# Ones through TensorE in the opening, maxima scaled on ScalarE, remainders of x on GpSimd

## The chip, the cores and the metric

The kernel runs on one core of a Trainium2 chip. The core has a matrix engine (TensorE, PE in the profile, with its weight loads PEld), three engines for elementwise work (VectorE or DVE, ScalarE or ACT, GpSimd or POOL), and a queue from which it issues DMAs (SyncE or SP). The metric is the device time of one execution in microseconds. The kernel before took 577.8 us as the median of three runs (575.98 to 578.51).

## The reference

Eight batches of windowed attention with 8 heads feed a mixing layer. Cut to what matters:

```python
scores = scale * np.matmul(q, k.transpose(0, 1, 3, 2))      # (8, 8, 576, 576), masked to a window
scores = scores - np.max(scores, axis=-1, keepdims=True)     # of 32 keys (plain, or every 4th of 128)
attn = np.exp(scores)
attn = attn / (np.sum(attn, axis=-1, keepdims=True) + 1e-09)
x = np.matmul(attn, v)                                       # heads side by side: (8, 576, 512)
theta = x @ w_theta
zr, zi = x * np.cos(theta), x * np.sin(theta)
y = np.einsum('ts,bsd->btd', w_tok_r, zr) + np.einsum('ts,bsd->btd', w_tok_i, zi)
u = x + y
out = u + np.maximum(u @ w_ch, 0.0)
```

q, k and v are fp32; the four weights are float64 in the kernel's inputs and are unpacked on the chip.

## The kernel before

**Stages.** A batch b has four pairs of heads. For a pair, `scores` multiplies blocks of 32 queries of both heads with the 64 keys in reach, into two PSUM banks (tag "s", two of them: a group of 5 blocks and one of 4), VectorE takes the row maxima, ScalarE the exponentials with their sums (line 485 or 504), VectorE the reciprocals of the sums (L507, L508) and GpSimd the product with them (L510). VectorE then transposes the probabilities in blocks of 32 (`turn`, L525; batch 0 does it on TensorE, `flip`), `pv` multiplies with v into the bank "v", ScalarE copies the result out as x (L581), and `x_split` makes from x a rounded part (ScalarE, L593) and a remainder (L597 for 64 columns, L599 for 512), since products are made in three passes of fp32r: rounded by rounded, rounded by remainder, remainder by rounded. `theta` multiplies x by w_theta, `trig` makes cosine and sine (L787 to L796, L698, L705), multiplies them by x (L750) and splits the results into zh (L641 or L644) and zl (L646). A `token` unit y(b, d, g) is 27 matmuls over nine z tiles (kt) for 128 channels d and half of the rows g; its sum is added to x (L825) and split again into u. A `chan` unit c(b, e, g) is 12 matmuls over u, added by L859.

**What overlaps.** From batch 1 on TensorE works on the units of one batch while the other engines make the probabilities, x, cosine and sine of the next. Names carry batch and pair: s1_2_0 is the first score group of batch 1, pair 2, xh1_0 the split x of batch 1, pair 0; the profile leaves the numbers out.

**The opening.** Up to about 144 us the kernel loads and unpacks the weights, does batch 0 whole and the attention of batch 1. A weight tile (st_wth, st_wtk, st_wch) is loaded as float64, clipped on VectorE (L332), scaled on ScalarE (L334, L340), joined on VectorE (L342), rounded on ScalarE (L350), and its remainder made on GpSimd (L352). The four tiles of w_ch, st_wch0 to st_wch3, take turns in two buffers, whose tags are xh2 and xh3: st_wch2 is loaded when GpSimd has made late_wc0 from st_wch0, st_wch3 when late_wc1 is made. Afterwards xh1_2 and xh1_3 live in the same buffers.

**What sets the order.** Batch 0 and batch 1's attention are written as tasks with ranks (`RANK`). A planner (`Order`) with a cost for each step and engine decides, when the kernel is built, in which order each engine takes them, and this order is then fixed. A cost in a `yield` therefore moves instructions when it changes. From phase(1, 2) on the order is that of the code. TensorE's matmuls go through `pe`, which keeps them in program order. In `row_max` (batch 0, and pairs (1,2), (1,3), (2,0), (2,1), whose mask is added by TensorE) the maxima are taken group by group (L430) and, behind batch 0, scaled by -1/8 on VectorE (L438); the exponentials of the group read them as bias.

## Time and profile before

| | |
|---|---|
| median of three runs | 577.8 us |
| profiled execution, its own time | 577.82 us |
| its span, first to last instruction | 576.0 us |
| busy share: TensorE, its weight loads | 96%, 87% |
| busy share: VectorE, ScalarE, GpSimd | 66%, 60%, 39% |
| mean granted clock of TensorE | 0.988 |

A row of the timeline is: start, duration, engine, line, operation, output<-input, shapes, count; in brackets the idle time before it and who ended it. Several instructions of one form in sequence stand in one row. A row by form has the busy time and the mean of one, then the idle time before. The clock is given as a share of 2.4 GHz. Since 200 us on look alike, nearly all that differs from a full TensorE lies in the first 145 us.

### The profile page before, as it was taken

What the parts mean: (1) busy time and instruction counts of PE and PEld (TensorE: products, weight loads), DVE (VectorE), ACT (ScalarE), POOL (GpSimd) and SP (SyncE); (2) the same over time, 40 slices, a digit from 0 to 9 for tenths busy, and PEclk for the clock granted to TensorE, in tenths of its full rate; (3) what the DMA queues carried; (4) which work ended last, traced back from release to release, by engine and by line L of the source; (5) the groups of instructions that cost most, each with busy time, mean ns of one, the idle gap of its engine ahead of it and who ended that gap; (6) DMA issues with size and microseconds to landing.
All of it is one profiled execution on the core that took longest, in us unless ns stands there. A gap on an engine that the chain in (4) does not pass through costs nothing.

```text
span 576.0 us, 13996 instructions
## 1 busy us (share of the span) xinstructions
PE 550.5 (96%) x5464; PEld 501.6 (87%) x5464; DVE 378.0 (66%) x1156; ACT 345.2 (60%) x939; POOL 222.2 (39%) x206
## 2 busy tenths in 40 slices
PE   5997799999999999999999999999999999999997
PEld 4744688879999899988999899988999899989997
DVE  3879798865666668756776768756775767445112
ACT  1498967768555784369555785359556695266110
POOL 2228855525224352226324253226323353325220
PEclk9999699899999999999999999999999999999999
DMA  8991437601747046540746146550747123321002
GB/s 303 400 368 28 165 105 245 216 0 63 231 150 193 32 162 210 169 127 20 268 143 172 64 148 202 181 136 11 252 146 190 69 83 102 77 89 65 18 1 83
DMA packets 45586, 81.91 MB, mean 142 GB/s; under 512 B 3920, under 2 KB 19024, under 8 KB 45520
## 3 DMA queue, kind: packets, MB, share of 16 engines
q1 hardware_dynamic: 45520, 81.02, 43.7%
q8 instruction: 43, 0.70, 0.5%
q14 instruction: 23, 0.19, 0.1%
HBM read 64.49 MB, written 16.52 MB: 141 GB/s over the span
## 4 chain that ended last, share of the span: by engine, by line
DVE 34%; ACT 30%; PE 25%; issue 5%; POOL 2%; DMA 2%; SPq 0%; ACTq 0%; POOLq 0%; DVEq 0%
DVE pt L525 16%; PE y L850 11%; ACT P L504 11%; PE c L882 6%; PE th L685 3%; DVE P L409 3%; ACT K L698 3%; ACT K L787 3%; DVE xh L599 3%; ACT th L796 2%; ACT zh L644 2%; DVE xq L729 2%; DVE K L789 2%; ACT cos L705 2%; ACT x L581 2%
## 5 line engine op out<-in xcount | busy, mean ns | idle before, releaser
L830 POOL TENSOR_TENSOR u<-x,u 128x288 fp32r<-128x288 f32 x64 | 54.7, 858 | 184.6 <-ACT u L828 184.6
L525 DVE STREAM_TRANSPOSE pt<-P 32x288 f32<-32x288 f32 x224 | 105.1, 469 | 12.0 <-POOL P L510 8.9
L882 PE MATMUL c<-u,late_wc 128*128 128x288 f32 x768 | 110.2, 296 | 2.8 <-DVE x L859 2.8
L882 PEld LDWEIGHTS c<-u,late_wc 128*128 128x128 f32 x768 | 106.0, 188 | 6.8 <-DVE x L859 4.0
L850 PE MATMUL y<-wtkh,zh 128*128 128x288 f32 x288 | 90.3, 314 | 1.1 <-ACT zh L644 1.1
L850 PE MATMUL y<-wtkh,zl 128*128 128x288 f32 x288 | 86.2, 299 | 4.0 <-POOL zl L646 4.0
L646 POOL TENSOR_TENSOR zl<-g,zh 128x512 fp32r<-128x512 f32 x40 | 52.3, 1316 | 97.5 <-ACT zh L644 84.5
L504 ACT ACTIVATE P<-P,mx 128x64 f32<-128x64 f32 x216 | 72.0, 335 | 25.8 <-DVE mx L498 25.8
L850 PE MATMUL y<-wtkl,zh 128*128 128x288 f32 x288 | 85.9, 298 | 0.0
L828 ACT CAST u<-x 128x288 fp32r<-128x288 f32 x64 | 26.9, 429 | 86.2 <-DVE x L825 85.5
L685 PE MATMUL th<-wthh,xh 128*128 128x512 f32 x224 | 74.8, 395 | 0.3 <-DVE g L784 0.3
L850 PE MATMUL y<-late_wt_b,zh 128*128 128x288 f32 x320 | 68.1, 297 | 0.0
L825 DVE TENSOR_TENSOR x<-y,x 128x288 f32<-128x288 f32 x64 | 28.1, 448 | 53.6 <-PE y L850 53.5
L850 PEld LDWEIGHTS y<-wtkh,zl 128*128 128x128 f32 x288 | 55.1, 191 | 4.7 <-POOL zl L646 4.7
L850 PEld LDWEIGHTS y<-wtkh,zh 128*128 128x128 f32 x288 | 54.9, 191 | 4.7 <-ACT zh L644 2.3
L850 PE MATMUL y<-late_wt_a,zh 128*128 128x288 f32 x256 | 56.3, 301 | 0.0
L850 PEld LDWEIGHTS y<-wtkl,zh 128*128 128x128 f32 x288 | 55.1, 191 | 0.3 <-issue 0.3
L510 POOL TENSOR_TENSOR P<-P,sm 128x576 f32<-128x576 f32 x32 | 37.5, 1172 | 41.1 <-DVE sm L508 18.1
L850 PEld LDWEIGHTS y<-late_wt_b,zh 128*128 128x128 f32 x320 | 51.4, 189 | 0.3
L685 PEld LDWEIGHTS th<-wthh,xh 128*128 128x128 f32 x224 | 42.0, 188 | 9.2 <-DVE g L784 0.6
L850 PE MATMUL y<-late_wt_b,zl 128*128 128x288 f32 x160 | 47.4, 296 | 0.0
L581 ACT COPY x<-o 128x576 f32<-128x576 f32 x32 | 29.4, 919 | 28.4 <-PE o L617 19.1
(108 smaller groups left out, 1106.3 us busy)
## 6 DMA issues: line engine op xcount, KB each, us to landing
q<-in_qT_dram SPq DMA_DIRECT2D x32, 576.0 KB, 5.2
va<-in_vw_dram SPq DMA_DIRECT2D x30, 320.0 KB, 3.2
k<-in_kT_dram SPq DMA_DIRECT2D x28, 304.0 KB, 5.5
out_dram<-x SPq DMA_DIRECT2D x28, 288.0 KB, 2.4
vb<-in_vw_dram SPq DMA_DIRECT2D x29, 256.0 KB, 3.8
xd<-xq SPq DMA_DIRECT2D x24, 288.0 KB, 5.1
xn<-xd SPq DMA_DIRECT2D x24, 256.0 KB, 3.4
st_wtk<-in_wtk_dram SPq DMA_DIRECT2D x8, 576.0 KB, 8.8
```

Source lines behind the costliest of these rows:

```text
L409: pin(nc.vector.tensor_tensor_reduce(out=P[:, n], in0=ps[:, n - g0], in1=mskb[:, mask_of(pr, n)], op0=ALU.add, op1=ALU.max, scale=1.0, sca ...
L504: table(nc.scalar.activation(P[:, n], P[:, n], AF.Exp, bias=mx[:, n:n + 1], scale=SCALE, accum_out=sm[:, n:n + 1]))
L510: pin(nc.gpsimd.tensor_tensor(P, P, sm.unsqueeze(2).to_broadcast([128, NJ, BW]), op=ALU.mult))
L525: pin(nc.vector.transpose(pmats[b, pr][k0:k0 + QB, :, hh, QB * e:QB * e + QB], P[p0:p0 + QB, :, QB * o:QB * o + QB]))
L581: pin(nc.scalar.copy(dst, src))
L646: pin(nc.gpsimd.tensor_tensor(lo, z, hi.bitcast(F32), op=ALU.subtract))
L685: pe(nc.tensor.matmul(pt, l, r, start=(n == 0), stop=(n == 3 * NC - 1)))
L825: pin(nc.vector.tensor_tensor(x[:, ts], ps, x[:, ts], op=ALU.add))
L828: pin(nc.scalar.copy(uh[b, d][:, ts], x[:, ts]))
L830: pin(nc.gpsimd.tensor_tensor(ul[b, d][:, ts], x[:, ts], uh[b, d][:, ts].bitcast(F32), op=ALU.subtract))
L850: pe(nc.tensor.matmul(ps, l[:, cs], r, start=(n == 0), stop=(n == 3 * NK - 1)))
L882: pe(nc.tensor.matmul(ps, l[:, cs], r[:, ts], start=(n == 0), stop=(n == 3 * NC - 1)))
```

## The change

It does five things. (1) Before the first loads arrive, VectorE writes a tile of ones, and TensorE multiplies it by itself 14 times (512 columns, bf16) into the bank of "v". (2) In unit (0,0,0), ahead of the tile kt = 3, it does so eight times before the first matmul and four times before the third, which needs the remainder. (3) In `row_max` the scaling of the maxima goes from VectorE to ScalarE, for the four pairs that are not of batch 0: eight instructions. (4) In `x_split` the remainders of pairs 0 to 2 of batch 1 go from VectorE to GpSimd, as those of pair 3 already are: six instructions. (5) As costs and engines of steps change, the planner sets another order for what follows, from the scores of (1,3) on.

```diff
--- before.py
+++ after.py
@@ -38,7 +38,10 @@
 
 FG0 = {4: ("zl2", "zl6"), 0: ("zl3", "zl7"), 1: ("zh3", "zh7")}
 COS_PSUM, SIN_PSUM = True, True
+WARM_UP = 14
 KORD = (0, 4, 1, 5, 2, 6, 3, 7, 8)
+
+KEEP_BUSY = {(0, 0, 0, 3, 0): 8, (0, 0, 0, 3, 2): 4}
 TP0 = {4: "s", 0: "s", 1: "x", 2: "t", 3: "s"}
 TP = {4: "t", 0: "s", 1: "s", 2: "t", 3: "s"}
 
@@ -434,8 +437,8 @@
                                         op=ALU.subtract))
             give(*rel)
         else:
-            yield "DVE", 170
-            pin(nc.vector.tensor_scalar(mx[:, g0:g1], mx[:, g0:g1], -SCALE, None, op0=ALU.mult))
+            yield "ACT", 220
+            pin(nc.scalar.mul(mx[:, g0:g1], mx[:, g0:g1], -SCALE))
         signal(key)
 
     def scores(b, pr):
@@ -591,7 +594,7 @@
         lo, lt = hl[:, S + 64:], hl[:, S:S + 64]
         yield "ACT", act(S)
         pin(nc.scalar.copy(hi, x))
-        on = pr < 3
+        on = pr < 3 and b > 1
         eng, cost = (nc.vector, dve) if on else (nc.gpsimd, pool)
         yield "DVE" if on else "POOL", cost(64)
         pin(eng.tensor_tensor(lt, x[:, FS:], hi[:, FS:].bitcast(F32), op=ALU.subtract))
@@ -845,10 +848,16 @@
             yield None, ("wtk", g, kt // 2)
             zh, zl = zs[b, kt]
             wh, wl = (w[:, HS * (kt % 2):HS * (kt % 2) + HS] for w in wtks[g, kt // 2])
+            if (b, d, g, kt) == (0, 0, 0, KORD[6]):
+                busy = yield from bank("v", "busy")
             yield "PE", 369
-            for l, r in ((zh, wh), (zh, wl), (zl, wh)):
+            for i, (l, r) in enumerate(((zh, wh), (zh, wl), (zl, wh))):
+                for _ in range(KEEP_BUSY.get((b, d, g, kt, i), 0)):
+                    pe(nc.tensor.matmul(busy[0][:, :DM], ones[:, :128], ones, start=True, stop=True))
                 pe(nc.tensor.matmul(ps, l[:, cs], r, start=(n == 0), stop=(n == 3 * NK - 1)))
                 n += 1
+        if b == d == g == 0:
+            give(*busy[1])
         signal(("tk", b, d, g))
         go(residual(b, d, g, ps, rel), RANK["evacuate"])
 
@@ -953,6 +962,12 @@
     EA, LA, LA2 = ([(t, reserve(t)) for t in ts] for ts in (EARLY, LATE, LATE2))
     XH = {p: reserve(f"xh{p}") for p in range(NP)}
     UH = {d: reserve(f"u{d}") for d in range(NC)}
+
+    ones = cp.tile([128, DM], BF16, name="ones")
+    nc.vector.memset(ones, 1.0)
+    busy = ps_v.tile([128, 2 * DM], F32, tag="v", name="busy")
+    for n in range(WARM_UP):
+        pe(nc.tensor.matmul(busy[:, :DM], ones[:, :128], ones, start=True, stop=True))
     od.live = True
     go(first_loads(), 0)
     go(consts(), 0)
```

VectorE at the scores of batch 1, pair 2. mx1_2 are the maxima, pt1 the transposed probabilities of pair 1, x0_2 the residual. Before:

```order
L430 TENSOR_REDUCE mx1_2_906<-s1_2_0_908 128x5
L525 STREAM_TRANSPOSE pt1_109<-P1_1_724 32x9x32 x2
L438 TENSOR_SCALAR mx1_2_906<-mx1_2_906 128x5
L430 TENSOR_REDUCE mx1_2_906<-s1_2_5_940 128x4
L825 TENSOR_TENSOR x0_2_407<-y0_2_0_883,x0_2_407 128x288
L438 TENSOR_SCALAR mx1_2_906<-mx1_2_906 128x4
```

And now:

```order
L433 TENSOR_REDUCE mx1_2_936<-s1_2_0_938 128x5
L528 STREAM_TRANSPOSE pt1_126<-P1_1_741 32x9x32 x2
L433 TENSOR_REDUCE mx1_2_936<-s1_2_5_970 128x4
L828 TENSOR_TENSOR x0_2_424<-y0_2_0_913,x0_2_424 128x288
L345 SCALAR_TENSOR_TENSOR st_wtk1_2_426<-st_wtk1_2_426 128x576
L345 SCALAR_TENSOR_TENSOR st_wtk1_3_496<-st_wtk1_3_496 128x576
```

The two scalings are gone; ScalarE has each of them directly ahead of the exponentials that read it.

GpSimd from the last product of batch 1 on (P1_3). xh1_n are the remainders of x, late_wcn the weights of the channel units, u0_n the remainders of batch 0's u. Before:

```order
L510 TENSOR_TENSOR P1_3_968<-P1_3_968,sm1_3_970 128x576
L830 TENSOR_TENSOR u0_0_831<-x0_0_274,u0_0_831 128x288
L352 TENSOR_TENSOR late_wc0_1205<-st_wch0_1063,late_wc0_1205 128x512
L352 TENSOR_TENSOR late_wc1_1231<-st_wch1_1113,late_wc1_1231 128x512
L830 TENSOR_TENSOR u0_1_884<-x0_1_350,u0_1_884 128x288
L510 TENSOR_TENSOR P2_0_1165<-P2_0_1165,sm2_0_1167 128x576
L352 TENSOR_TENSOR late_wc2_1373<-st_wch2_1233,late_wc2_1373 128x512
L352 TENSOR_TENSOR late_wc3_1383<-st_wch3_1262,late_wc3_1383 128x512
L830 TENSOR_TENSOR u0_2_957<-x0_2_407,u0_2_957 128x288
L510 TENSOR_TENSOR P2_1_1277<-P2_1_1277,sm2_1_1279 128x576
L597 TENSOR_TENSOR xh1_3_1454<-x1_3_1340,xh1_3_1454 128x64
L599 TENSOR_TENSOR xh1_3_1454<-x1_3_1340,xh1_3_1454 128x512
```

And now:

```order
L513 TENSOR_TENSOR P1_3_998<-P1_3_998,sm1_3_1000 128x576
L600 TENSOR_TENSOR xh1_0_1152<-x1_0_933,xh1_0_1152 128x64
L600 TENSOR_TENSOR xh1_1_1194<-x1_1_1076,xh1_1_1194 128x64
L602 TENSOR_TENSOR xh1_0_1152<-x1_0_933,xh1_0_1152 128x512
L602 TENSOR_TENSOR xh1_1_1194<-x1_1_1076,xh1_1_1194 128x512
L355 TENSOR_TENSOR late_wc0_1250<-st_wch0_1107,late_wc0_1250 128x512
L833 TENSOR_TENSOR u0_0_861<-x0_0_291,u0_0_861 128x288
L355 TENSOR_TENSOR late_wc1_1319<-st_wch1_1129,late_wc1_1319 128x512
L513 TENSOR_TENSOR P2_0_1175<-P2_0_1175,sm2_0_1177 128x576
L833 TENSOR_TENSOR u0_1_914<-x0_1_367,u0_1_914 128x288
L355 TENSOR_TENSOR late_wc2_1426<-st_wch2_1288,late_wc2_1426 128x512
L513 TENSOR_TENSOR P2_1_1301<-P2_1_1301,sm2_1_1303 128x576
```

Four remainders stand ahead of late_wc0, and P2_0 and P2_1 have moved forward; the two remainders of xh1_2 and those of xh1_3 follow behind late_wc3.

TensorE where batch 0's channel units (c0) meet theta of batch 1 (th1_4). Before:

```order
L882 MATMUL c0_0_0_1468<-u0_0_831,late_wc0_1205 128x288 x3
L882 MATMUL c0_0_0_1468<-u0_1_884,late_wc1_1231 128x288 x3
L882 MATMUL c0_0_0_1468<-u0_2_957,late_wc2_1373 128x288 x3
L882 MATMUL c0_0_0_1468<-u0_3_1121,late_wc3_1383 128x288 x3
L690 MATMUL th1_4_1477<-wthh0_631,xh1_0_1133 128x512
L692 MATMUL th1_4_1477<-wthl0_632,xh1_0_1133 64x512
L689 MATMUL th1_4_1477<-wthl1_654,xh1_1_1123 64x512
L690 MATMUL th1_4_1477<-wthh1_653,xh1_1_1123 128x512
L689 MATMUL th1_4_1477<-wthl2_673,xh1_2_1421 64x512
L690 MATMUL th1_4_1477<-wthh2_672,xh1_2_1421 128x512
L689 MATMUL th1_4_1477<-wthl3_685,xh1_3_1454 64x512
L690 MATMUL th1_4_1477<-wthh3_684,xh1_3_1454 128x512
```

And now:

```order
L891 MATMUL c0_0_0_1499<-u0_0_861,late_wc0_1250 128x288 x3
L891 MATMUL c0_0_0_1499<-u0_1_914,late_wc1_1319 128x288 x3
L891 MATMUL c0_0_0_1499<-u0_2_987,late_wc2_1426 128x288 x3
L891 MATMUL c0_0_0_1499<-u0_3_1125,late_wc3_1470 128x288 x3
L891 MATMUL c0_1_0_1519<-u0_0_861,late_wc0_1250 128x288 x3
L891 MATMUL c0_1_0_1519<-u0_1_914,late_wc1_1319 128x288 x3
L891 MATMUL c0_1_0_1519<-u0_2_987,late_wc2_1426 128x288 x3
L891 MATMUL c0_1_0_1519<-u0_3_1125,late_wc3_1470 128x288 x3
L891 MATMUL c0_2_0_1539<-u0_0_861,late_wc0_1250 128x288 x3
L693 MATMUL th1_4_1531<-wthh0_648,xh1_0_1152 128x512
L695 MATMUL th1_4_1531<-wthl0_649,xh1_0_1152 64x512
L692 MATMUL th1_4_1531<-wthl1_671,xh1_1_1194 64x512
```

The unit c0_1_0 and the first quarter of c0_2_0, 15 matmuls, now stand ahead of th1_4; the units behind move up, so that 12 fewer remain at the end.

## Rows read from the trace of the kernel before

**Rows 1.** Busy time by stretch: us, then PE, PEld, DVE, ACT, POOL, clock, DMA.

```profile
200.00:300.00 100.00, 98.91 (x1095) 93.44 (x1094) 71.42 (x259) 62.27 (x181) 37.06 (x34) 1.00 0.49 153
```

**Rows 2.** Timeline of TensorE, first scores.

```profile
10.27 1.34 PE L468 MATMUL s<-first_k,q 128*64 128x64 f32 x20
...
18.02 0.80 PE L468 MATMUL s<-first_k,q 128*64 128x64 f32 x20
```

**Rows 3.** Timelines of SyncE and VectorE, first st_wth, and its time to landing.

```profile
11.62 0.33 SPq L325 DMA_DIRECT2D st_wth<-in_wth_dram  x1
...
23.32 0.91 DVE L332 TENSOR_SCALAR st_wth<-st_wth 128x512 f32<-128x512 f32 x1
...
DMA to landing us min/median/max: 10.1/10.1/10.1
```

**Rows 4.** Busy time by stretch, two stretches at the lower clock.

```profile
67.82:71.24 3.42, 3.42 (x17) 3.42 (x16) 1.99 (x7) 3.42 (x17) 2.81 (x4) 0.50 0.00 0
101.95:105.37 3.42, 3.42 (x30) 2.89 (x30) 2.25 (x9) 2.19 (x10) 1.25 (x1) 0.50 0.84 275
```

**Rows 5.** Timeline of TensorE, its waits in the opening.

```profile
66.79 0.40 PE L850 MATMUL y<-wtkh,zl 128*128 128x288 f32 x1 [1.11 <-POOL zl L646]
...
82.47 0.31 PE L424 MATMUL s<-mskb,idb 128*128 128x64 bf16 x5 [1.04 <-ACT P L485]
...
101.51 0.30 PE L424 MATMUL s<-mskb,idb 128*128 128x64 bf16 x2 [1.95 <-ACT P L485]
...
125.11 0.63 PE L759 MATMUL xn<-idt,x 128*128 128x128 f32 x4 [1.02 <-DVE g L750]
```

**Rows 6.** VectorE by form from 80 to 116 us: busy us, mean ns.

```profile
L599 DVE TENSOR_TENSOR xh<-x,xh 128x512 fp32r<-128x512 f32 x3 | 2.1, 687 | 0.0
L438 DVE TENSOR_SCALAR mx<-mx 128x5 f32<-128x5 f32 x4 | 1.8, 455 | 0.1
...
L438 DVE TENSOR_SCALAR mx<-mx 128x4 f32<-128x4 f32 x4 | 1.2, 312 | 0.1
...
L597 DVE TENSOR_TENSOR xh<-x,xh 128x64 fp32r<-128x64 f32 x3 | 1.1, 363 | 0.0
```

**Rows 7.** Timelines of VectorE and ScalarE, scores of batch 1, pair 2.

```profile
79.02 0.49 DVE L430 TENSOR_REDUCE mx<-s 128x5 f32<-128x320 f32 x1
...
80.83 0.31 ACT L485 ACTIVATE P<-s,mx 128x64 f32<-128x64 f32 x1 [2.35 <-DVE mx L438]
```

**Rows 8.** Timelines of VectorE and GpSimd: a long scaling, weights, remainders.

```profile
84.77 1.30 DVE L438 TENSOR_SCALAR mx<-mx 128x5 f32<-128x5 f32 x1
...
84.60 1.45 POOL L352 TENSOR_TENSOR late_wt_b<-st_wtk,late_wt_b 128x576 fp32r<-128x576 f32 x1 [0.76 <-ACT late_wt_b L350]
...
109.70 2.60 POOL L352 TENSOR_TENSOR late_wc<-st_wch,late_wc 128x512 fp32r<-128x512 f32 x2 [2.27 <-ACT late_wc L350]
...
114.21 0.84 POOL L597 TENSOR_TENSOR xh<-x,xh 128x64 fp32r<-128x64 f32 x1
115.01 1.30 POOL L599 TENSOR_TENSOR xh<-x,xh 128x512 fp32r<-128x512 f32 x1
116.27 0.81 POOL L830 TENSOR_TENSOR u<-x,u 128x288 fp32r<-128x288 f32 x1
```

**Rows 9.** The load of st_wch3: time to landing, and VectorE's first use.

```profile
DMA to landing us min/median/max: 5.6/5.6/5.6
...
105.36 0.43 DVE L332 TENSOR_SCALAR st_wch<-st_wch 128x512 f32<-128x512 f32 x1 [1.03 <-DMA st_wch<-in_wch_dram]
```

**Rows 10.** Timelines of TensorE and VectorE, end of the opening.

```profile
116.34 0.40 PE L690 MATMUL th<-wthh,xh 128*128 128x512 f32 x1
...
138.84 4.24 PE L882 MATMUL c<-u,late_wc 128*128 128x288 f32 x30
143.01 1.27 PE L468 MATMUL s<-k,q 128*64 128x64 f32 x36
...
143.86 0.22 DVE L409 CUSTOM_DVE_ANT_0 P<-s,mskb 128x64 f32<-128x64 f32 x1 [0.28 <-PE s L468]
```

## Prediction

> **What bounds the kernel now.** I read the busy time by stretch first: from 200 to 300 us TensorE is busy 98.91 of 100 us [rows 1]. The body is bound by TensorE and its work is untouched, so what the opening gives or costs, up to where batch 1's token units begin (about 144 us), comes through to the end one for one. Second, TensorE's timeline, to see where it runs slowly. The first scores of a pair, 20 matmuls, take 1.34 us at 10.27 and 0.80 at 18.02 [rows 2]; the duration says that the clock stands at its lower level (1.2 GHz) in the first, though no change of clock is recorded before it. Two later stretches of 3.42 us stand at a granted 0.50 [rows 4]; each can cost at most half of itself, 1.7 us. Third, TensorE's waits: 1.11 us for the last zl, 1.04 and 1.95 us for a score bank that ScalarE's exponentials hold, 1.02 us for a multiplication at 125 [rows 5]. The low stretches of 67.82 and 101.95 come right behind the waits that end at 66.79 and 101.51; behind the single wait of 1.04 there is none. Last, who makes TensorE wait: ScalarE had been idle for 2.35 us when the exponentials began at 80.83, for want of a scaled maximum whose reduction had begun at 79.02 [rows 7]. That is VectorE's queue.
>
> **Fourteen matmuls of ones at the start.** The trace has none; 30 channel matmuls of 288 columns take 4.24 us, 0.14 each [rows 10], so 512 columns should take about 0.25 at the higher level and 0.50 at the lower: 3.5 to 7 us, from about 1.3, beside the first loads. If the clock then stands at 2.4 GHz, the second pair still waits for its load until 10.27, but each group behind saves 0.54 us (1.34 less 0.80): two more pairs and a flip up to 17 us make about 1.8. Then the weights decide. The first st_wth is issued at 11.62 and lands 10.1 us later, about 21.9 counted from the end of the issue; VectorE uses it at 23.32 [rows 3]. So about 1.4 us passes this point. Behind it the elementwise engines work in a fixed order from loads that are there, and I carry the 1.4 through. Bounds: 0 (the clock falls again while pair 1 is awaited, some 1.2 us, which lies between the wait of 1.04 that left it up and that of 1.95 that did not) and -1.8. I take **-1.4**, since 1.2 is nearer to 1.04.
>
> **Twelve matmuls of ones in unit (0,0,0).** Eight ahead of kt 3's zh and four ahead of its zl, each lot in a wait of 1.1 us. At 0.25 they take 2.0 and 1.0 us, so zl's matmul starts about 0.5 us late, and the low stretch at 67.82 goes (up to 1.7 of TensorE's time). Neither reaches the end by itself: VectorE gets the unit's sum before its next transposes are ready either way, and what TensorE wins until 81 it waits away at the bank of 82.47. At the lower level the twelve take twice as long and the first residual is about 1 us late. I take **0**, bounds -0.3 and +1.0.
>
> **Eight scalings to ScalarE, six remainders to GpSimd.** VectorE loses 1.8 + 1.2 us of L438 and 2.1 + 1.1 us of L597 and L599 [rows 6], 6.2 us where it is the engine that others wait for. A scaling on ScalarE has no row; the nearest, an exponential over 64 columns, is 0.31 [rows 7], a bound from above, and I take 0.25. It can start where the reduction ends (79.5), not behind two transposes, so the exponentials and the bank come about 0.9 us earlier. TensorE gains the waits of 1.04 and 1.95 and the low stretches, up to 1.7 each, 6.4 in all; some 2.2 come back as waits, since it arrives earlier at the first bank than the bank does (1.9) and just ahead of the second (0.3), and 0.4 is the late zl: it reaches the channel units about 3.8 us earlier.
>
> But these need more than TensorE. st_wch3 goes into the buffer of st_wch1, once GpSimd has made late_wc1. It lands 5.6 us after its issue, and VectorE waits 1.03 us for it, until 105.36 [rows 9]; late_wc3 ends at 112.30 [rows 8]. In the new order four remainders (2 x 0.84 + 2 x 1.30 = 4.3 us) stand on GpSimd ahead of late_wc0, and on ScalarE the cast for late_wc1 stands behind nine exponentials and a copy. Taking what is queued in turn, I get late_wc1 1.0 to 2.4 us later than now. Its load then shares the queue with less, and so lands sooner after its issue: late_wc3 ends about where it does now, 111.0 to 113.5. Behind it GpSimd then has two pairs of remainders and one u, 2 x 2.14 + 0.8 = 5.1 us, where it had 4.0 (115.01 + 1.30 less 112.30) [rows 8]. The last matmul of th1_4, at 116.34 [rows 10] right behind GpSimd's last remainder, so moves **later by 1.0**, bounds -0.3 and +2.4.
>
> What remains behind that matmul gets shorter. Now it is 143.01 - 116.34 = 26.7 us to the next scores. Fifteen channel matmuls now stand ahead of th1_4: 15 x 0.14 = 2.1 us. The wait of 1.02 and a short one ahead of it go, 1.3, since VectorE's queue is then empty and takes th1_4 at once. Against this the last multiplication by a cosine stands behind five score masks, 5 x 0.15 us from start to start (0.22 each) [rows 10], and its remainder ends about 0.8 us after TensorE wants it. Tail: -2.1 - 1.3 + 0.8 = **-2.6**.
>
> Sum: -1.4 + 0 + 1.0 - 2.6 = -3.0 on the profiled execution's span of 576.0; with the 1.8 us around it that execution took 577.8, the median of the three. **574.8 us.**
>
> **A rule against the change.** VectorE's scaling at 84.77 took 1.30 us, as long as GpSimd's subtraction from 84.60 went on (1.45) [rows 8]; the mean of its kind is 0.46 [rows 6]. The page "SBUF — State Buffer" of the Trainium skill (section "Who interferes with whom") says that VectorE's two-port operations, tensor_scalar among them, and GpSimd's take a shared pair of ports as a lock for a whole instruction. The trace agrees, as far as that row goes. By that rule each of the four L332 of st_wch could wait out a remainder of 1.30, and the sum would be up to 5 us worse, an estimate of about 580. Rival (c) is the same danger, worked out from rows.
>
> **Rivals.** (a) The ones do not do what they say: the clock falls again before pair 1, the first term is 0, 576.2. For it: only matmuls of 64 columns follow, and the wait of 1.2. Against it: the wait of 1.04 did no harm. (b) The weights' chain does not bind: st_wch3 lands early, GpSimd keeps up, and the 3.8 us reach the end: -3.8 - 1.3 + 0.8 - 1.4 = -5.7, 572.1. For it: GpSimd is the least busy engine. Against it: ScalarE's queue ahead of late_wc1. (c) Slower: GpSimd's queue becomes the bound. The four remainders (4.3) come whole in front of late_wc1, and the L332 of st_wch1 and of st_wch3 wait 1.3 each behind a remainder: late_wc3 6.9 later, the last matmul of th1_4 8.0 later, +8.0 - 2.6 - 1.4 = +4.0, 581.8. It decides when GpSimd's last remainder of batch 1 ends after 120.3 (no gain left) and is slower from 123.2. For it: the 1.30 at 84.77. Against it: GpSimd stands idle in front of most of these rows now.
>
> **How the numbers follow.** About half a per cent, 2.9 us, is what a measurement of this kernel can tell from no change; the border is 574.9. Forecast 0.50, some 573.0 to 576.4, half of it on either side of the border; (a) 0.16; (b) 0.22; (c) 0.12. Faster 0.22 + 0.25 = 0.47; same 0.25 + 0.16 = 0.41; slower 0.12. The range leaves out (c) and the far end of (b): 571.0 to 578.0.
>
> **What would show it.** Right: score groups of 0.80 at 10.27; the first st_wth used near 21.9; no low stretch around 68; exponentials of (1,2) right behind their reduction; the last matmul of th1_4 near 115.9 (117.3 less 1.4), behind a remainder on GpSimd; the scores of (2,2) near 139. Wrong: groups of 1.34 at 10.27; GpSimd idle ahead of its last remainders, or with a queue there past 120; a new low stretch behind a wait for late_wc3 around 110, which I have not priced and which could cost up to 1.7.

## The result, and the profile after

The changed kernel takes 580.25 us, the median of 7 runs (578.66 to 580.83), against 577.45 for the kernel before (7 runs, 575.98 to 578.51): a ratio of 1.0046 with a 95% interval of 1.0033 to 1.0059. It is slower by about 2.7 us, where 574.8 was forecast and the range ended at 578.0. The profiled execution took 579.98, its span is 578.2, 2.1 more than that of before.

To see where the 2.1 us come from I set the start of the same instruction in the two traces side by side; "later" and "earlier" below are such differences, counted from each span's start. At the score group that starts at 18.02 in before TensorE is 1.9 earlier (16.13), VectorE uses the first st_wth 0.9 earlier, and at 31 us both are 0.3 later. VectorE is still 0.2 to 0.3 later at 81. The last matmul of th1_4 is 4.6 later, the scores of pair (2,2) 0.9. From 156 us on VectorE is 2.1 later. TensorE is 1.3 later there, since it waits less on the way, and 2.1 later only from 206 us to the end (its wait for a residual there is 0.89, in before 0.52). So the whole loss is made ahead of 156 us, and VectorE's queue carries it into the body [rows 1], which passes it on unchanged from 206 us.

**The start.** TensorE's timeline, which answers [rows 2] and [rows 3]. Columns: start, duration, engine, line, operation, tiles, count, and in brackets the idle time ahead with what ended it ("issue": nothing that the profile shows).

```profile
1.45 5.83 PE L970 MATMUL busy<-ones 128*128 128x512 bf16 x14 [1.45 <-DVE halfpi L306]
...
10.19 0.80 PE L471 MATMUL s<-first_k,q 128*64 128x64 f32 x20 [0.60 <-DMA first_k<-in_kT_dram]
...
16.76 0.86 PE L620 MATMUL o<-pt,first_v 128*64 128x64 f32 x22
18.78 0.62 PE L620 MATMUL o<-pt,first_v 128*64 128x64 f32 x14 [1.16 <-issue]
19.34 0.80 PE L564 MATMUL pT<-idt,P 64*64 64x64 f32 x20
20.07 0.29 PE L427 MATMUL s<-mskb,idb 128*128 128x64 bf16 x4
20.29 0.68 PE L564 MATMUL pT<-idt,P 64*64 64x64 f32 x16
20.90 0.69 PE L471 MATMUL s<-first_k,q 128*64 128x64 f32 x16
21.41 1.22 PE L620 MATMUL o<-pt,first_v 128*64 128x64 f32 x36
23.11 0.91 PE L564 MATMUL pT<-idt,P 64*64 64x64 f32 x22 [0.48 <-POOL P L513]
24.91 0.67 PE L564 MATMUL pT<-idt,P 64*64 64x64 f32 x14 [0.89 <-issue]
```

The ones do what they say: the score groups take 0.80. But TensorE then stops twice in the middle of 36 equal matmuls, behind the 22nd, for 1.16 and 0.89 us. Between the two stops lie 14 + 20 + 4 + 16 + 16 + 36 + 22 = 128 matmuls, each with a weight load of its own: 256 instructions. The queues (queue, kind: packets, MB, share of the DMA engines), first for 15.9 to 17.6 us, then for the whole span:

```profile
q1 hardware_dynamic: 271, 0.66, 99.5%
q8 instruction: 1, 0.02, 3.9%
```

```profile
q8 instruction: 43, 0.70, 0.5%
```

One packet of instructions is on its way just ahead of the first stop, beside loads that fill the DMA engines; another lies in 22.4 to 23.9 us, and none between 18 and 22. Over the span 43 packets of 16 KB stand against 5490 matmuls and 5490 loads, which is 255 for each. So in these traces TensorE's instructions come in packets of 256, and beside the first loads it waits for the next one. TensorE's waits list two such stops in the whole span, these two; in before none.

**Unit (0,0,0).** The last zl's matmul starts at 67.17, against 66.79 [rows 5]; the low stretch of 67.82 [rows 4] is gone, and TensorE runs into the banks at 78.34 (0.76 idle) and 81.81 (1.02 idle). VectorE is where it was.

**The weights' chain**, which answers [rows 8], on GpSimd:

```profile
97.08 1.31 POOL L355 TENSOR_TENSOR late_wc<-st_wch,late_wc 128x512 fp32r<-128x512 f32 x1 [1.67 <-ACT late_wc L353]
...
102.21 1.30 POOL L355 TENSOR_TENSOR late_wc<-st_wch,late_wc 128x512 fp32r<-128x512 f32 x1 [3.06 <-ACT late_wc L353]
...
108.28 1.30 POOL L355 TENSOR_TENSOR late_wc<-st_wch,late_wc 128x512 fp32r<-128x512 f32 x1 [2.54 <-ACT late_wc L353]
...
113.96 1.28 POOL L355 TENSOR_TENSOR late_wc<-st_wch,late_wc 128x512 fp32r<-128x512 f32 x1
...
117.76 1.27 POOL L602 TENSOR_TENSOR xh<-x,xh 128x512 fp32r<-128x512 f32 x1
```

Before, late_wc0 and late_wc1 were made one behind the other:

```profile
96.73 2.86 POOL L352 TENSOR_TENSOR late_wc<-st_wch,late_wc 128x512 fp32r<-128x512 f32 x2 [0.33 <-ACT late_wc L350]
```

late_wc1 now ends at 103.51, 3.9 later; the load of st_wch3, which waits for it, is issued at 103.54 instead of 99.6, and late_wc3 ends at 115.24, 2.9 later. GpSimd is idle ahead of three of the four and waits for casts on ScalarE. Only late_wc3 itself stands behind a queue there: its cast ended at 112.95, and GpSimd first made a product and a remainder of u, 1.0 us (0.8 in before). ScalarE's rows for st_wch0 and st_wch1, of before and then of after:

```profile
94.50 0.70 ACT L334 ACTIVATE st_wch<-st_wch 128x512 f32<-128x512 f32 x1 [1.74 <-DVE st_wch L332]
...
95.99 0.66 ACT L350 CAST late_wc<-st_wch 128x512 fp32r<-128x512 f32 x1
...
97.18 0.67 ACT L350 CAST late_wc<-st_wch 128x512 fp32r<-128x512 f32 x1 [0.53 <-DVE st_wch L342]
```

```profile
96.34 0.67 ACT L353 CAST late_wc<-st_wch 128x512 fp32r<-128x512 f32 x1 [1.01 <-DVE st_wch L345]
96.91 0.68 ACT L337 ACTIVATE st_wch<-st_wch 128x512 f32<-128x512 f32 x1
...
101.47 0.67 ACT L353 CAST late_wc<-st_wch 128x512 fp32r<-128x512 f32 x1
```

The first step on st_wch1 (L334, now L337) stood ahead of the cast for late_wc0 and now stands behind it: 94.50 becomes 96.91. VectorE's next step (L345) comes at 100.22, behind a reduction and two transposes, and the cast behind a copy and four exponentials at 101.47, 4.3 later than before.

One more step on this chain became long, VectorE's clip of st_wch3 (L335, L332 of before), and ScalarE was idle for it:

```profile
108.49 1.39 DVE L335 TENSOR_SCALAR st_wch<-st_wch 128x512 f32<-128x512 f32 x1
109.95 0.67 ACT L337 ACTIVATE st_wch<-st_wch 128x512 f32<-128x512 f32 x1 [1.75 <-DVE st_wch L335]
```

It took 0.43 in before; here it runs beside GpSimd's subtraction for late_wc2 (108.28 to 109.58). So what st_wch3 won by landing sooner, 4.6 us behind its issue and not 5.6, the clip lost again.

**What TensorE makes of it**, which answers [rows 10] and [rows 4]: its timeline, then busy time by stretch (stretch, length, busy time and count of PE, PEld, DVE, ACT, POOL, then granted clock, DMA share, GB/s).

```profile
111.90 1.63 PE L891 MATMUL c<-u,late_wc 128*128 128x288 f32 x11
115.29 4.16 PE L891 MATMUL c<-u,late_wc 128*128 128x288 f32 x16 [1.76 <-POOL late_wc L355]
...
120.97 0.39 PE L693 MATMUL th<-wthh,xh 128*128 128x512 f32 x1
...
143.87 1.27 PE L471 MATMUL s<-k,q 128*64 128x64 f32 x36
```

```profile
116.05:119.47 3.42, 3.42 (x16) 3.42 (x15) 2.46 (x6) 0.23 (x1) 2.98 (x4) 0.50 0.00 0
```

Before, all twelve matmuls of the first channel unit went through at once:

```profile
113.14 1.74 PE L882 MATMUL c<-u,late_wc 128*128 128x288 f32 x12
```

TensorE now comes to the channel units 1.2 earlier (111.90 against 113.14), does what it can, waits 1.76 for late_wc3, and behind that wait 3.42 us stand at a granted 0.50, the lower level. Counted to the last matmul of th1_4: 1.2 earlier, the wait 1.76, half of the slow stretch 1.7, and the 15 channel matmuls that now stand ahead, 2.1, make 4.4 of the 4.6.

**The cosine.** VectorE and ScalarE behind the scores of (2,2):

```profile
145.45 0.69 DVE L753 TENSOR_TENSOR K<-xn,K 128x512 f32<-128x512 f32 x1
...
146.17 0.62 ACT L647 CAST zh<-K 128x512 fp32r<-128x512 f32 x1 [1.30 <-DVE K L753]
```

In before the cast waited less:

```profile
142.64 0.62 ACT L644 CAST zh<-K 128x512 fp32r<-128x512 f32 x1 [0.25 <-DVE K L750]
```

The multiplication now starts behind five masks. VectorE's loss goes from 0.86 at the scores to 2.11 at 156 us, 1.25; TensorE's reaches 2.12 at 206.

### The profile page after: what moved, and what is told of

It is laid out like the page before. It is cut to its first block, busy times and chain, and to the rows that moved or that the text cites. A ratio compares the mean times of both kernels' runs of the same rounds, so it can differ in the third digit from the quotient of the medians.

```text
span 578.2 us, 14049 instructions
## 1 busy us (share of the span) xinstructions
PE 555.3 (96%) x5490; PEld 501.3 (87%) x5490; DVE 374.7 (65%) x1143; ACT 345.8 (60%) x947; POOL 225.8 (39%) x212
## 4 chain that ended last, share of the span: by engine, by line
DVE 27%; ACT 26%; PE 23%; issue 3%; POOL 2%; ACTq 0%; DVEq 0%; POOLq 0%
DVE pt L528 13%; ACT P L507 10%; PE y L857 10%; PE c L891 7%; PE th L688 4%; DVE P L412 3%; ACT K L701 3%; ACT th L799 2%; DVE xh L602 2%; ACT K L790 2%; ACT zh L647 2%; DVE xq L732 2%; ACT cos L708 2%; DVE K L792 2%; ACT x L584 1%
## 5 line engine op out<-in xcount | busy, mean ns | idle before, releaser
L891 PE MATMUL c<-u,late_wc 128*128 128x288 f32 x768 | 112.3, 299 | 5.0 <-DVE x L868 3.2
L891 PEld LDWEIGHTS c<-u,late_wc 128*128 128x128 f32 x768 | 107.6, 190 | 9.4 <-DVE x L868 4.3
```

What stands on the lines that cost most here:

```text
L891: pe(nc.tensor.matmul(ps, l[:, cs], r[:, ts], start=(n == 0), stop=(n == 3 * NC - 1)))
```

## The experiments

The theory after the comparison (A): the loss has two places, the late late_wc3 (a wait, and the clock that falls behind it) and the cosine behind the masks; the ones at the start gain nothing since instructions stop TensorE there. Rival (B): one of the four parts costs it all, or the order of the instructions as a whole does. Every kernel here computes the whole reference. "of before" is the median of the runs of before that were made beside it. The changed kernel was not run again beside the experiments. The before that ran beside it took 577.45, the one beside other kernels up to 578.81, so a kernel is set against the changed one by the two ratios; where the intervals of two ratios overlap, as most here do, the order of the two is not shown.

### Each part alone

e_warm, the ones at the start:

```diff
+WARM_UP = 14
...
+    ones = cp.tile([128, DM], BF16, name="ones")
+    nc.vector.memset(ones, 1.0)
+    busy = ps_v.tile([128, 2 * DM], F32, tag="v", name="busy")
+    for n in range(WARM_UP):
+        pe(nc.tensor.matmul(busy[:, :DM], ones[:, :128], ones, start=True, stop=True))
```

e_keep, the ones in the unit:

```diff
+KEEP_BUSY = {(0, 0, 0, 3, 0): 8, (0, 0, 0, 3, 2): 4}
...
+                for _ in range(KEEP_BUSY.get((b, d, g, kt, i), 0)):
+                    pe(nc.tensor.matmul(busy[0][:, :DM], ones[:, :128], ones, start=True, stop=True))
```

e_scale and e_rem, the scalings and the remainders:

```diff
-            pin(nc.vector.tensor_scalar(mx[:, g0:g1], mx[:, g0:g1], -SCALE, None, op0=ALU.mult))
+            pin(nc.scalar.mul(mx[:, g0:g1], mx[:, g0:g1], -SCALE))
```

```diff
-        on = pr < 3
+        on = pr < 3 and b > 1
```

> The kernel before with the fourteen matmuls of ones at the start alone. In the changed kernel TensorE was 1.9 us ahead at 17 us and then stood idle for 1.16 us in the middle of the group that starts at 16.76 and for 0.89 us in the middle of the one at 23.11, with nothing it waited for; 256 of its instructions lie between the two places, and each comes about 1.2 to 1.5 us behind the end of a packet of its instruction queue (16 KB, 256 instructions). Theory A (TensorE runs out of instructions, since the packets stand behind the loads): the same two gaps here, VectorE's first L345 at 26.6 as in the changed kernel (26.31 before), time +0.3 us, 577.4 to 578.2. Rival B (the prediction's step: 1.4 us pass the first weights, and are lost only further on through other parts of the change): first L345 near 24.9, time -1.4, 575.5 to 576.5.

> The kernel before with the twelve matmuls of ones in unit (0,0,0) alone. Theory A (they take the low stretch at 67.8 away, but what TensorE wins is waited away at the next score bank, and VectorE's queue does not move): VectorE's maxima of (1,2) at 79.0 as before, TensorE waits about 2.3 us at the bank of 82.47, time within 0.5 us of before. Rival B (TensorE's 1.3 us reach the units of 100 us): the scores of batch 2, pair 2, at 141.7 instead of 143.0, time -1.3 us.

> The kernel before with the eight scalings on ScalarE alone; remainders stay on VectorE. In the changed kernel the remainder late_wc1 was made 3.9 us later than before (its end 103.5, before 99.6), so the last weight tile was issued 3.9 us later and late_wc3 ended at 115.24 (before 112.30). Theory A (the order that the planner makes when the scalings move puts the weight steps behind other work on VectorE and ScalarE; GpSimd stood idle ahead of late_wc0 and late_wc1): the same here, late_wc1 ends 2.5 us or more later than before, TensorE waits for late_wc3 at its first channel unit and has a low clock behind it, time +1 to +3 us. Rival B (the remainders on GpSimd do it: four of them ahead of late_wc0, and the clips of 1.0 and 1.4 us beside GpSimd): late_wc1 ends at 99.6 to 101, no wait for late_wc3, time -1 to -4 us.

> The kernel before with the six remainders of x on GpSimd alone; scalings stay on VectorE. Theory A (order by the scalings): the weights' chain stays about where it was, late_wc1 ends at 99 to 101.5, no wait of TensorE for late_wc3 of over 0.5 us, time -1 to +0.5 us. Rival B (the remainders on GpSimd delay the weights): late_wc1 ends at 103 or later, a wait for late_wc3 and a low stretch behind it, time +1 to +3 us.

Medians 579.73, 579.73, 579.86 and 579.83 (of before 577.3); ratios 1.0039 (1.0023 to 1.0055), 1.0037 (1.0022 to 1.0052), 1.0047 (1.0032 to 1.0062) and 1.0040 (1.0026 to 1.0053). Each part alone costs 2.4 to 2.6 us, nearly as much as all four. The costs don't add, and most of what I expected of the single parts was wrong: e_warm's time lies in neither range, and only its second stop for instructions is there (0.49, behind the 22nd matmul); e_keep waits 1.54 us at the bank of 82 us where about 2.3 was expected.

The scalings alone already make late_wc1 end at 104.1 and late_wc3 at 114.4, and TensorE shows the picture of the changed kernel, in four waits instead of one, with a low stretch of its own:

```profile
116.00 3.11 PE L885 MATMUL c<-u,late_wc 128*128 128x288 f32 x12 [1.13 <-DVE x L828]
```

```profile
116.19:119.60 3.41, 3.41 (x14) 3.16 (x14) 2.27 (x5) 0.22 (x1) 1.31 (x2) 0.50 0.00 0
```

The remainders alone leave late_wc1 where it was (99.1). Their trace, the fastest of its ten runs, shows the cosine's 1.25, from 0.77 earlier at 143 us to 0.48 later at 156; late_wc3 ends 1.8 later there too (114.09), but no wait for it follows. The rest of their median I can't place. So the remainders alone cost about as much while late_wc1 stays in time.

With ones alone the loss comes between 88 and 110 us, at another place. TensorE and VectorE of e_keep:

```profile
103.30 0.43 PE L427 MATMUL s<-mskb,idb 128*128 128x64 bf16 x2 [3.46 <-ACT P L488]
```

```profile
92.55 0.43 DVE L335 TENSOR_SCALAR st_wch<-st_wch 128x512 f32<-128x512 f32 x1 [1.23 <-DMA st_wch<-in_wch_dram]
...
109.49 0.42 DVE L433 TENSOR_REDUCE mx<-s 128x4 f32<-128x256 f32 x1 [2.36 <-PE s L471]
```

```profile
102.45:109.28 6.83, 5.98 (x51) 5.15 (x50) 4.10 (x13) 5.43 (x24) 2.40 (x2) 0.50 0.55 202
```

The first st_wch lands 5.9 us after its issue (4.6 in before), VectorE waits for it, the scores of (2,0) get their bank 3.46 us late, the clock falls, and VectorE then waits 2.36 for scores made at the lower level. e_warm shows the same chain (6.2, 1.47, 3.70, 1.33). Why this tile lands later there is not settled.

### A second trace of the ones at the start

> The kernel with the ones at the start alone, unchanged, for a second trace. Theory A (TensorE stands idle for instructions behind the 22nd matmul of the two groups in most executions, and the head start is gone by 35 us; what is left of the loss lies between 88 and 110 us): idle behind the 22nd of both groups, level with the kernel before within 0.5 us at 35 us, 1 us or more behind it at 115 us. Rival B (the loss lies at the start or in the body): more than 0.5 us behind at 35 us, or growing behind 150 us.

581.23 in its one run. The clock fell again from 11.39 to 18.22, no stop for instructions showed, and TensorE was not ahead. The chain of 88 to 110 us is there again: 6.2 to landing, then 1.52, 3.76 and 1.14. So that chain doesn't hang on the head start; the head start itself is not certain either. From 31 to 143 us this trace is about 2 us later than that of e_warm, whose order it has (1.92 and 2.15).

### Nothing changed, and ones without a matmul

> The kernel before once more, with nothing changed, as a kernel of its own. Each part of the change alone cost 2.4 to 2.6 us, which neither theory of any part gave. Theory A (each part costs something of its own): 577.3 us, ratio 1.000, and its trace shows by how much the opening differs from one execution to the next. Rival B (the time of this kernel depends on when and where it is run, not on the parts): 579.5 us or more.

> The kernel before with only the tile of ones in SBUF and VectorE's write to it, and no matmul of ones. The two parts with matmuls of ones have this tile in common. Theory A (the tile costs nothing, since VectorE is idle until 8 us): 577.3 us within 0.5. Rival B (the tile moves what lies behind it in SBUF, or the write delays something, and that is what costs 2.4 us in both): 579.3 to 580.0.

578.76 and 578.25 (of before 578.22): 1.0010 (0.9994 to 1.0027) and 1.0003 (0.9986 to 1.0020). The tile and its memset cost nothing. e_same is the kernel before, and its trace is the more useful one: here, by its durations, the clock rose in the second score group, while before still needs 1.34 for a group at 13.63, and TensorE was 1.6 earlier at the group of 18.02 without a single matmul of ones.

```profile
10.09 1.15 PE L468 MATMUL s<-first_k,q 128*64 128x64 f32 x20 [0.24 <-DMA first_k<-in_kT_dram]
...
13.14 0.80 PE L468 MATMUL s<-first_k,q 128*64 128x64 f32 x20
```

Part of this goes at the places where the changed kernel stops for instructions:

```profile
17.39 1.15 POOL L510 TENSOR_TENSOR P<-P,sm 128x576 f32<-128x576 f32 x1 [2.93 <-ACT pt L539]
```

```profile
19.31 0.80 PE L561 MATMUL pT<-idt,P 64*64 64x64 f32 x20 [1.07 <-POOL P L510]
```

The product that TensorE is said to wait for ends at 18.54, 0.77 ahead of the transposes; in before they follow the same product by 0.06 (20.17 to 20.23). The second stop ends at 25.83, 0.9 behind the copy of pt that the matmuls read (24.92; in before they follow it by 0.05). Of the 1.6, VectorE has 0.9 left from 24 to 102 us, and nothing behind 110; TensorE has 0.9 from 52 to 118.7, and nothing behind 120.3. VectorE:

```profile
105.39 0.43 DVE L332 TENSOR_SCALAR st_wch<-st_wch 128x512 f32<-128x512 f32 x1 [2.06 <-DMA st_wch<-in_wch_dram]
```

VectorE waits 2.06 for the last st_wch where it waited 1.03 [rows 9]; both traces go on at the same time. In before's order a head start at the beginning is lost in that wait, and there the prediction's "comes through to the end one for one" fails. In the changed kernel's order it holds, as far as traces of equal order show: e_no_ones is 0.17 ahead of the changed kernel at 31 us and 0.13 at 570; e_moves_mended is 2.2 ahead of e_both at 81 us and 2.1 at 570; e_fill_wc is 1.15 ahead of e_both at 81 and 1.11 at 143, where their orders part.

### Without the ones, without the remainders

e_no_ones has the scalings and the remainders alone; e_no_rem is the changed kernel with this:

```diff
-        on = pr < 3 and b > 1
+        on = pr < 3
```

> The changed kernel without either lot of ones: scalings on ScalarE and remainders on GpSimd together. Theory A (the weights' chain in this order is late by itself: late_wc1 ends at 103 or later, TensorE waits for late_wc3 at its channel units): 579.5 to 581. Rival B (the ones, which let TensorE run further ahead, bring about the wait and the low clock behind it): late_wc1 ends by 101.5, no wait of over 0.5 us for late_wc3, 576.5 to 578.

> The changed kernel with the remainders of batch 1 back on VectorE: ones in both places and scalings on ScalarE. Theory A (order by the scalings): a wait for late_wc3 at the first channel units, 579.5 to 581. Rival B (remainders on GpSimd hold up the weights): no such wait, 575 to 577.5.

579.63 and 580.96: 1.0030 (1.0013 to 1.0047) and 1.0052 (1.0031 to 1.0074). Without any ones the loss stays, with the wait of 1.76 and a low stretch at 115.70. Without the remainders it stays too, in four waits as in e_scale (0.20, 0.86 and 0.83 for late_wc, then 1.13 for a residual), with a low stretch behind them. What both have in common is the scalings. They make the late chain, and the ones are not needed for it.

### The two places mended

e_fill_wc puts eight ones ahead of the matmuls of the first channel unit that read late_wc3; e_cos_first takes the fixed place in VectorE's queue from the masks of (2,2)'s first five scores, so that the cosine is multiplied ahead of them; e_both does both.

```diff
+            if (b, e, g, c) == (0, 0, 0, 3):
+                for _ in range(8):
+                    pe(nc.tensor.matmul(fill[:, :DM], ones[:, :128], ones, start=True, stop=True))
```

```diff
+        keep = pin if (b, pr, g0) != (2, 2, 0) else pe
...
-            pin(nc.vector.tensor_tensor_reduce(
+            keep(nc.vector.tensor_tensor_reduce(
```

> The changed kernel with eight more matmuls of ones in the first channel unit, ahead of the three matmuls that need late_wc3. There TensorE waited 1.76 us and then did 16 channel matmuls in 4.16 us, at half the clock. Nothing else moves on any engine. Theory A (the clock that falls behind this wait costs the time: TensorE is what ends last from here to the next scores): no low stretch at 116, the channel matmuls behind the wait at 0.14 us each, the scores of (2,2) 1.5 to 1.9 us earlier, 578.4 to 579.0 where the changed kernel has 580.3. Rival B (what ends last here is GpSimd, whose last remainder of batch 1 ended at 119.0): the low stretch goes, th1_4 still ends at 120.5 or later, 579.8 to 580.5.

> The changed kernel with VectorE's last multiplication by a cosine ahead of the score masks of (2,2) again, where it stood before; the transposes behind it move by one place too. In every run with another order the time from the scores of (2,2) to the second residual of batch 1 was 1.25 us longer than before. Theory A (that is the cost of the place behind five masks): these 1.25 us come back, 578.9 to 579.3 where the changed kernel has 580.3. Rival B (it only moves the masks back by as much): within 0.4 of the changed kernel.

> The changed kernel with both: eight ones ahead of the matmuls that need late_wc3, and the multiplication by the cosine ahead of the masks. Theory A (clock and place are separate losses on one path): the sum of the two single gains, about 2.7 to 3.1 us, 577.2 to 577.7. Rival B (the next thing in line takes the gain): 578.5 or more.

579.64, 579.16 and 578.82 (of before 578.11): 1.0024 (1.0011 to 1.0037), 1.0020 (1.0003 to 1.0037) and 1.0007 (0.9991 to 1.0024). By the middles of the ratios each takes back about half of the change's 1.0046, though e_fill_wc's and e_cos_first's intervals overlap that of the change; with both no difference from before can be measured. e_fill_wc's time lies between A's range and B's, and e_both's 578.82 lies in B's by itself and in A's only by the ratio. The traces of e_fill_wc and e_cos_first bear A out: what the changed kernel loses, it loses at these two places. In e_fill_wc the stretch stays at the full clock, and at the scores of (2,2) it is 0.05 later than before where the changed kernel is 0.86; the 1.3 at 570 us are then the cosine's. The gain is 0.8 of the 1.5 to 1.9 expected, since behind it the next wait is for a residual.

```profile
112.93 1.90 PE L894 MATMUL fill<-ones 128*128 128x512 bf16 x7
114.48 2.98 PE L897 MATMUL c<-u,late_wc 128*128 128x288 f32 x15
118.06 0.66 PE L897 MATMUL c<-u,late_wc 128*128 128x288 f32 x3 [0.60 <-DVE x L868]
```

```profile
112.00:119.00 7.00, 6.22 (x36) 4.52 (x36) 5.15 (x12) 1.84 (x4) 6.94 (x8) 1.00 0.00 0
```

In e_cos_first TensorE's loss grows by 0.57 behind the scores of (2,2), from 0.29 to 0.86 at 206 us, instead of by 1.26, since the cast waits 0.25 and not 1.30:

```profile
144.55 0.62 ACT L648 CAST zh<-K 128x512 fp32r<-128x512 f32 x1 [0.25 <-DVE K L754]
```

The trace of e_both shows rival (a) as it was told: the clock is up behind the ones and falls again while pair 1 is awaited, 1.39 us; its low stretch is 12.92 to 16.34, and it is 2.0 later than before at 31 us. Its median is level with before all the same.

```profile
10.62 0.80 PE L472 MATMUL s<-first_k,q 128*64 128x64 f32 x20 [1.39 <-DMA first_k<-in_kT_dram]
...
13.45 1.34 PE L472 MATMUL s<-first_k,q 128*64 128x64 f32 x20
```

### The ones of the unit, with their later wait filled

In e_keep's kernel, ahead of the first scores of (2,0):

```diff
+                for _ in range(14 if at else 0):
+                    pe(nc.tensor.matmul(fill[:, :DM], ones[:, :128], ones, start=True, stop=True))
```

> The run with the twelve ones in unit (0,0,0) alone, and in it fourteen more ones ahead of the first scores of batch 2, where TensorE had waited 3.46 us for a bank and then stood at the low clock from 102.5 to 109.3. Nothing else moves. Theory A (TensorE that arrives earlier waits longer at this bank, loses its clock, and VectorE then waits 2.4 us for the scores): no low stretch behind 102, VectorE's wait of 2.36 under 0.8, 577.6 to 578.6 where the run without had 579.7. Rival B (the loss lies ahead of it, in weight tiles that land later): VectorE's clip of the first st_wch as late as 92.5, 579.2 to 580.

579.24 (of before 578.11): 1.0023 (1.0005 to 1.0040). There is no low stretch behind 102, the wait at the bank is 0.68, and the 2.36 on VectorE is gone. The lag is 2.52 at 102 and 1.28 at 110 us, where e_keep has 1.78 and 2.99. The clock that falls behind the bank's wait was a good part of that loss in this trace. The time itself lies in B's range, and the first st_wch lands late here too (6.2).

### Other numbers of instructions at the start

e_warm with five ones of four bytes, and with eight large ones and 38 of 64 columns:

```diff
-WARM_UP = 14
+WARM_UP = 5
...
-    ones = cp.tile([128, DM], BF16, name="ones")
+    ones = cp.tile([128, DM], F32, name="ones")
```

```diff
-WARM_UP = 14
+WARM_UP = 8
...
+    for n in range(38):
+        pe(nc.tensor.matmul(busy[:, :64], ones[:, :128], ones[:, :64], start=True, stop=True))
```

> As the run with ones at the start alone, but with five matmuls of fp32 ones instead of fourteen of bf16: about the same time on TensorE, 10 instructions instead of 28. Theory A (TensorE runs out of instructions at every 256th): the places where it stands idle without waiting for data come nine matmuls later in the program, behind the 31st of the 36 matmuls of o and of the transposes, where they came behind the 22nd; the time within 0.5 us of that run's (579.7), since the packets come no earlier. Rival B (the idle time belongs to the data of that group): still behind the 22nd, or none.

> As the run with ones at the start alone, but with eight matmuls of 512 columns and 38 of 64 columns: 92 instructions instead of 28, in about the same time. Theory A: the places come 32 matmuls earlier than behind the 22nd of the o group, that is in the score group ahead of it (10 of its matmuls later), and likewise 10 matmuls ahead of the transposes at 23 us. Rival B: at the same place as with 28, or none.

e_warm_few: 578.45 (of before 578.0), 1.0002 (0.9992 to 1.0011), where a time near e_warm's 579.7 was expected. If the stops come at fixed counts of instructions, fewer ones move them to later matmuls. The five stand in the trace as ten matmuls, 20 instructions with their loads, not the 10 that I had counted; the old 14 made 28. So the stop should move by (28 - 20) / 2 = 4 matmuls, and it does, at both places, from the 22nd to the 26th. e_same has none of these instructions, which makes it 28 / 2 = 14 matmuls, and its stops stand behind the 36th at both places:

```profile
17.59 0.98 PE L620 MATMUL o<-pt,first_v 128*64 128x64 f32 x26
19.77 0.51 PE L620 MATMUL o<-pt,first_v 128*64 128x64 f32 x10 [1.20 <-issue]
...
23.98 1.02 PE L564 MATMUL pT<-idt,P 64*64 64x64 f32 x26 [0.48 <-POOL P L513]
25.91 0.56 PE L564 MATMUL pT<-idt,P 64*64 64x64 f32 x10 [0.90 <-issue]
```

It is 1.17 later than before from 31 to 102 us and only 0.10 from 110 us on: in before's order a late start is lost there just as an early one. e_warm_many, one run of 578.44, had the clock fall again from about 11 to 18 us and no stop at all; it tells nothing on the count.

### A third buffer for w_ch

If the load of st_wch3 need not wait for late_wc1, its lateness should cost nothing.

```diff
-LATE2 = ("xh2", "xh3", "xh2", "xh3")
+LATE2 = ("xh2", "xh3", "sw0", "xh2")
```

> The kernel before with a third buffer for the tiles of w_ch: st_wch2 is loaded at once into its own, st_wch3 follows st_wch0. The planner makes another order of this. Theory A (the opening is tied to the landing of the last w_ch tiles, at 105.4 in both runs of the kernel before): VectorE's wait for the last tile goes, and the scores of (2,2) come 1 to 3 us earlier, 575 to 577 if the order does no harm elsewhere. Rival B (VectorE's and ScalarE's own queue sets the pace, the wait for the tile is filled with what comes behind it): 577.3 to 579.

> The changed kernel with a third buffer for the tiles of w_ch. Theory A (its weights' chain is late for want of a buffer): late_wc3 is made before 108, no wait of TensorE for it, no low stretch behind it, and with the cosine ahead of the masks in this order, 575.5 to 577.5. Rival B (the queues set the pace): late_wc3 after 112, 578.5 to 580.5.

In the kernel before: 579.33 (of before 578.0), 1.0030 (1.0013 to 1.0047); in the changed one 579.23, 1.0018 (1.0002 to 1.0034). In the latter late_wc3 starts at 111.52 instead of 113.96, and neither the wait for it nor the low stretch is there; but it ends at 112.84, as B said, and not before 108. Its trace still ends 2.1 later than before, as the changed kernel's does; its first stop for instructions took 1.86 us, and it is 1.0 later at 31 us already. In the former, whose time lies above both ranges, late_wc3 starts at 109.68, and TensorE waits somewhere else:

```profile
119.34 1.85 PE L882 MATMUL c<-u,late_wc 128*128 128x288 f32 x12 [1.25 <-DVE x L825]
```

So B holds some truth: these edits let the planner set another order, and another order than that of before has mostly cost 1 to 2 us somewhere else.

### The two moves, mended, without the ones

> Scalings on ScalarE and remainders on GpSimd as in the changed kernel, the eight ones ahead of the matmuls that need late_wc3, the cosine ahead of the masks; no ones at the start and none in unit (0,0,0). Theory A (the moves cost what the two repairs undo, and the other ones bring nothing): the 579.6 of both moves less the 2.2 that the repairs brought in the changed kernel, 577.0 to 577.7, ratio 0.998 to 1.000. Rival B (without the other ones TensorE is too late for the place where the eight stand, and they delay it): 578.3 or more, ratio over 1.001.

Scalings and remainders moved, the wait for late_wc3 filled, the cosine ahead of the masks, no ones at the start or in the unit: 578.91 (of before 578.81), 1.0006 (0.9994 to 1.0019); the time lies in B's range, the ratio between A's and B's. Nothing that I ran beats the kernel before.

## Why the prediction was wrong

**The step that failed is the sentence "late_wc3 ends about where it does now, 111.0 to 113.5".** It ends at 115.24. What leads up to it was too low already: late_wc1 came 3.9 later, not 1.0 to 2.4. I had followed the last cast through ScalarE's queue, but not the two steps ahead of it, which had also moved back in ScalarE's and VectorE's. And the load was to land sooner and give it all back; it gave back 1.0, which the long clip of st_wch3 took again. Behind it the wait of 1.76 and the low stretch of 3.42 us came as the last sentence of the prediction named them without a price. The term "+1.0" has measured +4.6 on the last matmul of th1_4; of this 2.1 are the 15 channel matmuls, which the tail gets back. That matmul was not set by GpSimd's last remainder, as the prediction had it: the remainder ended at 119.03, 2.7 later than before, and the work behind late_wc3 took 3.8 there instead of 5.1, since a remainder of 64 columns takes 0.31 and not 0.84. TensorE came to the matmul at 120.97, held up by its own slow stretch.

**The start, -1.4:** wrong in this trace, +0.3 at 31 us. The clock came as forecast and 1.9 us were won by 16; two stops for instructions, which no row of before shows, took it back. This, and not the carrying, is what failed in the changed kernel, whose order carries a start to the end. In before's order even a start that was kept (e_warm, 1.5 up to 88 us; e_same, 0.9) didn't reach it. That the clock stayed up in the wait for pair 1 was in part luck: it did behind 0.60 and fell behind 1.39 (e_both), but it also stayed up behind 1.02 in e_third_buffer_all, and in before a low stretch follows a wait of 1.11 (to 66.79), so waits of 1.04 and 1.95 were no tight bounds. Ones at the start also gain less than I thought since the clock rises by itself in the second score group in some executions without them (e_rem, e_same).

**Unit (0,0,0), 0:** right in this trace, since what TensorE gained by 75 us was waited away by 82. But e_keep shows that the twelve alone cost 0.37%, through the chain of 88 to 110 us, which the bounds of -0.3 to +1.0 did not hold.

**Scalings and remainders:** ScalarE's scaling took 0.21 where 0.25 was taken, and the exponentials of (1,2) came 0.7 earlier (80.17). TensorE reached the channel units 1.2 earlier, not 3.8.

**The tail, -2.6:** right in sum. The last matmul of th1_4 is 4.63 late and VectorE 2.11 at 156 us, TensorE 2.12 from 206: -2.5. The cosine in it cost 1.25, not 0.8; the rest made good for it.

**The range.** It left out all above 578.0, though the one unpriced sign (a wait for late_wc3, up to 1.7) lay on the path and the bound of late_wc3 was no bound. Taking the far end of late_wc1's own range, 2.4, through to late_wc3 would have put the term at +3.4 instead of +1.0 and the time at 577.2, and the slow stretch at 578.9.

**The rivals.** (c)'s time, 581.8, came nearer than the forecast, by luck, since most of the loss was made elsewhere. GpSimd's queue was no bound: it was idle for 1.67 + 3.06 + 2.54 us ahead of three of the four late_wc, and its last remainder of batch 1 ended at 119.03, under the 120.3 from which (c) would decide. (c)'s other half, a clip that waits out GpSimd, happened once on the path. The clip is L335 now, L332 before, and stands four times on the chain, once for each st_wch; two of the four were long (1.02 at 94.68 and 1.39 at 108.49, against 0.54 and 0.49), both beside a GpSimd subtraction, and in before one was, beside a product of GpSimd's (1.00, against 0.43). The two are 1.0 us longer in sum than the one and a short one of before. By the rule of the Trainium skill, page "SBUF — State Buffer", section "Who interferes with whom", VectorE and GpSimd can shut each other out here. The trace agrees with that rule of the Trainium skill, at a fifth of the 5 us estimated from it; that the estimate's 580 is nearest of all to 580.25 is luck as well. In e_scale and e_no_rem the clip of st_wch3 takes 0.42 and 0.43, and late_wc3 ends at 114.41 and 114.70, sooner than here although late_wc1 ends 0.6 and 0.9 later; that the clip alone does this is not shown, since their remainders are VectorE's. (b) is refuted: the chain bound. (a) happened in some executions, as e_both shows.

**What stays open:** why the first st_wch lands about 6 us after its issue in the kernels with 14 ones at the start or 12 in the unit, and 3.8 to 4.9 in all others (e_warm, e_warm_again, e_keep and e_keep_fill have 5.9 to 6.2; the changed kernel, with both, has 4.3); what of the remainders' median lies outside the cosine; and why the costs of the single parts don't add.

## What to carry to other kernels

A gain at the start of a kernel is worth only what is left of it behind the next load that everyone waits for, and whether there is such a load depends on the order (here in before's, not in the changed one's); compare the same instruction in two traces at several points before carrying a term to the end. When work moves between engines, follow the longest chain of small steps that crosses them (here load, clip, cast, subtraction, next load) through every queue in its new order, and don't let a transfer "give back" what its issue lost. Price every wait that you name as a danger: one of 1.8 us here brought 3.4 us at the lower clock with it, and filling it gave back 0.8.

## What the runs showed that was not expected

- TensorE's instructions come in packets of 16 KB, one for each 256 instructions (43 packets for the 10,980 of matmuls and loads). With the loads at a DMA share of about 1.0 from 10 to 40 us a packet came late enough to stop TensorE 0.3 to 1.9 us (after: 1.16 and 0.89, and never again in its span). The stops show only where TensorE is early, with ones or without. Without ones the row names another engine, since a wait is put down to whoever released last: e_same stops 0.8 and 0.9 behind its last input, behind the 36th matmul where 28 instructions fewer put it.
- The clock's first rise varies from run to run of one kernel: in e_same the second score group takes 1.15 and the third 0.80, in before the third still 1.34. It was worth 1.6 us at 16 us and nothing at the end. With ones it can fall again (e_both, e_warm_again).
- A stretch at the lower clock costs only where others wait for TensorE: before has one (101.95 to 105.37) behind its wait of 1.95 us for the bank, e_same has none behind 1.97, and VectorE goes on at 105.4 in both. In e_keep, behind 3.46, VectorE then waits 2.36 for scores.
- Four edits that cost 2.4 to 2.6 us each cost 2.7 together (1.0037 to 1.0047 each, 1.0046 together).
